# Scores of sliding-window attention: three one-bank PSUM tiles and a shared bank in place of two two-bank tiles

## The chip, the cores and the metric

One core of a Trainium2 chip runs the whole program. The metric is the device time of one execution in microseconds (us), lower is better. PE is TensorE (matmuls), DVE is VectorE, ACT is ScalarE, POOL is GpSimd, SP is SyncE, whose queue issues most of the DMAs. PSUM, into which PE writes, has eight banks of 512 fp32 columns for each partition, and this program uses all eight.

## The reference

Two independent layers whose outputs are put side by side: attention with a sliding window of 256 keys, and a Fourier mixing layer made of matrix products.

```python
q, k, v = (x @ wqkv)                      # 2048 tokens, 32 heads of 32
scores = q @ k.T * 32 ** -0.5
mask = (idx[:, None] - idx[None, :] >= 0) & (idx[:, None] - idx[None, :] < 256)
p = softmax(where(mask, scores, -1e9))
a = (p @ v) @ wo
b = dft_seq_re @ (xb @ dft_hid_re.T) - dft_seq_im @ (xb @ dft_hid_im.T)
out = concatenate([a, b], axis=-1)
```

## The kernel before

Every large product is made of fp16 matmuls on high and low halves of the fp32 operands, three passes each (`PASSES`). The first third of the program computes q, k and v; then come the products of the Fourier layer ("x" units, then "c" units by `seven`, four times over), and the output projection closes it.

Attention runs as a generator, `attention`, that is mixed into these products: each product calls `tick` after every 4 or 8 matmuls, and at a fixed rate the generator advances by one step. One block is a query block of 128 tokens and a pair of heads; there are 256 blocks, numbered b, ordered by head group, 512-token chunk, head pair and query block. `mm` chains all of these matmuls, so PE's order is the order in which the code is written, save for the small transposes (`pt_...`) behind the scale factors. DVE, ACT and SP order comes from the scheduler of the build, which simulates the program.

A block goes through these steps (lines of the profile):

- `s_step` (L205 to L249): PE writes the scores of two heads into a PSUM tile `s` (L222). A query block sees three key blocks: the two last ones, and the first one, of which the window cuts off one triangle, exactly the complement of the causal triangle of the diagonal block. So DVE copies the first key block's scores over the masked triangle of the diagonal block (L230, "the copy"); two key blocks' width is left. DVE takes the negative maximum (L232, `mx`), ACT makes the bias (L235), ACT writes the exponentials back into `s` (L242, one per head), ACT makes the high halves `hi` (L245), and DVE the low halves `lo` (L246), both into the tile `hl`. A transposing DMA (L248) turns `hl` into `t`.
- `z_step` (L260, L262), three blocks later, on POOL: the merged triangle is split again.
- `v_step`, `LAG` = 6 blocks later: PE multiplies by the values into `pv`; DVE normalises.

The tile `s` is 2 x 512 fp32, two banks, one per head, of which 3 x 128 columns each are used. The pool `ps_s` has two of them, so the matmuls of block b write where block b-2 stood, whose last reader is L246 on DVE. The first two query blocks of a sequence have one or two key blocks and no first key block to fold in; there the copy takes a constant (`never2`). Key blocks come from 512-token chunks (`k2s`, four key blocks each); a run of key blocks that crosses a chunk's edge needs two matmuls, one that does not needs one.

Around it, DVE also makes the low halves of the other operands (L115), the combinations of operands (L635) and of results (L683, L828).

## Time and profile before

| | |
|---|---|
| three runs | 1811.86, 1812.89, 1817.40 us; median 1812.89 |
| the profiled execution: its time | 1813.55 us |
| the profiled execution: its span, first to last instruction | 1811.5 us |
| mean granted TensorE clock | 0.989 |
| matmuls | 10876, of which 704 are scores (L222, recorded under the helper's line L108) |
| DMA | 297.95 MB, mean 164 GB/s |

The profile is one execution recorded by the hardware. A page sums each engine's busy time, groups instructions by line, operation and tile, and names what ended the idle time before them; other views list the waits, the chain of work that ended last, and the instructions in order of time. The helper `mm` stands at L108, so matmuls are told apart by tile names, with buffer numbers left out: `s` is the score tile, `p`, `p_a`, `p_b` and `p_c` are the Fourier products. In the timeline, rows read: start in us, duration in us, engine, line, operation, output<-input, shape, count of merged instructions, and in brackets the idle time before it and what ended it.

### The profile page before, as it was taken

What the parts mean: (1) busy time and instruction counts of PE and PEld (TensorE: products, weight loads), DVE (VectorE), ACT (ScalarE), POOL (GpSimd) and SP (SyncE); (2) the same over time, 40 slices, a digit from 0 to 9 for tenths busy, and PEclk for the clock granted to TensorE, in tenths of its full rate; (3) what the DMA queues carried; (4) which work ended last, traced back from release to release, by engine and by line L of the source; (5) the groups of instructions that cost most, each with busy time, mean ns of one, the idle gap of its engine ahead of it and who ended that gap; (6) DMA issues with size and microseconds to landing.
All of it is one profiled execution on the core that took longest, in us unless ns stands there. A gap on an engine that the chain in (4) does not pass through costs nothing.

```text
span 1811.5 us, 30024 instructions
## 1 busy us (share of the span) xinstructions
PE 1751.8 (97%) x10876; PEld 854.7 (47%) x10876; DVE 1327.5 (73%) x2362; ACT 1103.1 (61%) x1867; POOL 423.8 (23%) x666
## 2 busy tenths in 40 slices
PE   7999999999999999999989999999999989997999
PEld 3444445555555544554444444444444544443444
DVE  7666787777766788886788887779777778586542
ACT  3233555456555777876778876678776767563222
POOL 0000222122212232332244343324442234000000
PEclk9999999999999999999999999999999999998999
DMA  5357998978866666877657999847999747744431
GB/s 232 124 166 212 222 252 214 230 177 210 195 141 164 137 132 158 188 193 193 125 116 174 207 190 199 170 97 155 189 187 180 150 85 135 217 93 78 132 94 70
DMA packets 440596, 297.95 MB, mean 164 GB/s; under 512 B 339072, under 2 KB 396416, under 8 KB 440448
## 3 DMA queue, kind: packets, MB, share of 16 engines
q1 hardware_dynamic: 433536, 270.87, 63.8%
q0 software_dynamic: 6912, 25.17, 8.0%
q8 instruction: 85, 1.39, 0.3%
q14 instruction: 63, 0.52, 0.1%
HBM read 146.93 MB, written 75.63 MB: 123 GB/s over the span
## 4 chain that ended last, share of the span: by engine, by line
PE 75%; DVE 14%; ACT 5%; issue 3%; DMA 2%; POOL 0%; SPq 0%; ACTq 0%; DVEq 0%; POOLq 0%
PE p_a L108 12%; PE pv L108 12%; PE p L108 11%; PE pk L108 9%; PE pq L108 9%; PE p_b L108 6%; PE po_a L108 5%; PE s L108 4%; PE p_c L108 3%; PE po_b L108 2%; DVE reg L683 2%; DVE mx L232 1%; DVE raw_u L635 1%; PE po_c L108 1%; DVE reg L115 1%
## 5 line engine op out<-in xcount | busy, mean ns | idle before, releaser
L108 PE MATMUL p<-reg,un 128*128 128x512 f16 x1536 | 353.3, 382 | 2.5 <-ACT reg L826 2.5
L242 ACT ACTIVATE s<-s,bias,escs 128x256 f32<-128x256 f32 (+1 forms) x512 | 270.0, 527 | 12.2
L235 ACT ACTIVATE bias<-mx,pshift,escs 128x2 f32<-128x2 f32 x256 | 98.3, 384 | 258.4 <-DVE mx L232 257.6
L239 POOL TENSOR_SCALAR mark<-bias 128x1 f32<-128x1 f32 x128 | 46.5, 363 | 831.9 <-ACT bias L235 816.2
L108 PEld LDWEIGHTS <-un 128*128 128x128 f16 x1536 | 147.3, 98 | 167.2 <-issue 8.0
L246 DVE TENSOR_TENSOR hl<-s,hl 128x512 f16<-128x512 f32 (+1 forms) x256 | 170.1, 664 | 73.8 <-ACT hl L245 72.4
L262 POOL TENSOR_SCALAR_AFFINE_SELECT t<-t 128x512 f16<-128x512 f16 x224 | 184.9, 891 | 0.1
L108 PE MATMUL pq<-reg,wu_q 128*128 128x512 f16 x768 | 176.7, 385 | 7.5 <-ACT reg L121 4.3
L108 PE MATMUL p_a<-reg,un_c 128*128 128x512 f16 x768 | 182.8, 383 | 0.0
L108 PE MATMUL pk<-reg,wu_k 128*128 128x512 f16 x768 | 174.6, 379 | 0.0
L108 PE MATMUL pv<-reg,reg 128*128 128x512 f16 x768 | 174.0, 379 | 0.0
L260 POOL TENSOR_SCALAR_AFFINE_SELECT z<-t 128x512 f16<-128x512 f16 x224 | 164.2, 754 | 41.4 <-DMA t<-hl 37.7
L232 DVE TENSOR_REDUCE mx<-s 128x2 f32<-128x512 f32 (+1 forms) x256 | 170.8, 667 | 3.3
L108 PEld LDWEIGHTS <-reg 128*128 128x128 f16 x1152 | 110.1, 97 | 121.8
L245 ACT ACTIVATE hl<-s 128x512 f16<-128x512 f32 (+1 forms) x256 | 148.9, 582 | 9.8 <-DMA t<-hl 3.8
L230 DVE COPY_PREDICATED s<-upper,s 128x256 f32<-128x256 uint32 x224 | 94.5, 422 | 72.7 <-PE s L108 72.3
L108 PE MATMUL s<-qk,qk 96*128 96x128 f16 (+2 forms) x704 | 121.7, 276 | 15.4 <-DVE hl L246 14.7
L108 PEld LDWEIGHTS <-un_b 128*128 128x128 f16 x768 | 73.3, 98 | 101.4 <-issue 11.4
L108 PEld LDWEIGHTS <-wu_q 128*128 128x128 f16 x768 | 74.9, 99 | 95.6 <-issue 13.2
L108 PEld LDWEIGHTS <-un_c 128*128 128x128 f16 x768 | 74.4, 99 | 86.3 <-issue 4.4
L108 PEld LDWEIGHTS <-un_a 128*128 128x128 f16 x768 | 73.8, 97 | 84.7 <-issue 5.8
L108 PEld LDWEIGHTS <-wu_k 128*128 128x128 f16 x768 | 73.4, 97 | 81.1
(174 smaller groups left out, 2855.7 us busy)
## 6 DMA issues: line engine op xcount, KB each, us to landing
raw_u<-in_cs_dram SPq DMA_DIRECT2D x64, 512.0 KB, 4.4
qk<-qs SPq DMA_DIRECT2D x192, 128.0 KB, 3.2
out_dram<-y POOLq DMA_DIRECT2D x36, 512.0 KB, 7.8
raw_u<-in_xb_dram SPq DMA_DIRECT2D x32, 512.0 KB, 4.0
vs<-yv SPq DMA_DIRECT2D x32, 260.0 KB, 2.7
vt<-vs SPq DMA_DIRECT2D x32, 260.0 KB, 3.4
raw_x<-in_xa_dram SPq DMA_DIRECT2D x16, 512.0 KB, 10.2
qs<-yq SPq DMA_DIRECT2D x32, 256.0 KB, 2.4
```

The costliest lines, as they stand in the source:

```text
L108: fixed[:] = [nc.tensor.matmul(*args, **kwargs)]
L115: latest[:] = [f(*args, **kwargs)]
L230: nc.vector.copy_predicated(s[:, :, 2 * P:3 * P], upper2, s[:, :, :P] if nb == 3 else never2)
L232: nc.vector.tensor_reduce(mx, sv, axis=AX.X, op=ALU.max, negate=True)
L235: nc.scalar.activation(bias, mx, AF.Identity, bias=pshift, scale=es)
L239: marks[:] = [nc.gpsimd.tensor_scalar(mark, bias[:, 0:1], 1.0, None, op0=ALU.mult)]
L242: nc.scalar.activation(sv[:, h], sv[:, h], AF.Exp, bias=bias[:, h:h + 1], scale=es)
L245: nc.scalar.activation(hi, sv, AF.Copy)
L246: behind[:] = [nc.vector.tensor_tensor(lo, sv, hi, op=ALU.subtract)]
L260: nc.gpsimd.affine_select(out=z, in_=pk, compare_op=ALU.is_gt, fill=0.0, base=0, pattern=[[0, 4], [-1, P]], channel_multiplier=1)
L262: nc.gpsimd.affine_select(out=pk, in_=pk, compare_op=ALU.is_ge, fill=0.0, base=0, pattern=[[0, 4], [1, P]], channel_multiplier=-1)
L683: nc.vector.tensor_tensor(lo, src, hi, op=ALU.subtract)
```

## The change

The score tile becomes one bank: 2 heads x 256 columns, for the last two key blocks. There are three of them in place of two. The first key block gets a tile of its own, `far`, one bank for the whole program, 2 x 2 x 128 columns: one half for even blocks and one for odd ones, and in each half one part per head. The matmuls of a head are cut where the chunk ends, as before, and now also between the first key block and the two last ones. The copy reads from `far` and writes into `s`. The sum of banks stays at eight.

```diff
-    ps_s_cm = tc.tile_pool(name="ps_s", bufs=2, space=PSUM)
+    ps_s_cm = tc.tile_pool(name="ps_s", bufs=3, space=PSUM)
...
+        far = ps_s.tile([P, 2, 2, P], F32, tag="far", bufs=1, name="far")
...
-                st[b] = {"s": ps_s.tile([P, 2, 512], F32, tag="s", name=f"s_{b}")}
+                st[b] = {"s": ps_s.tile([P, 2, 2 * P], F32, tag="s", name=f"s_{b}")}
+                if nb == 3:
+                    st[b]["far"] = far[:, b % 2]
...
-            k0 = qb + 1 - nb
-            while k0 <= qb:
-                k1 = min(qb + 1, (k0 // QB + 1) * QB)
-                at = (k0 - (qb - 2)) * P
-                mm(s[:, j, at:at + (k1 - k0) * P], q2s[g, sc][:, h, i * P:i * P + P],
-                                 k2s[g, k0 // QB][:, h, k0 % QB * P:k0 % QB * P + (k1 - k0) * P],
-                                 start=True, stop=True, skip_group_check=True)
-                k0 = k1
+            edges = [k for k in range(qb + 1 - nb, qb + 2) if k in (qb + 1 - nb, qb - 1, qb + 1) or k % QB == 0]
+            for k0, k1 in zip(edges, edges[1:]):
+                at = (k0 - (qb - 1)) * P
+                mm(d["far"][:, j] if at < 0 else s[:, j, at:at + (k1 - k0) * P],
+                   q2s[g, sc][:, h, i * P:i * P + P],
+                   k2s[g, k0 // QB][:, h, k0 % QB * P:k0 % QB * P + (k1 - k0) * P],
+                   start=True, stop=True, skip_group_check=True)
...
-            sv = s[:, :, 3 * P - w:3 * P]
-            nc.vector.copy_predicated(s[:, :, 2 * P:3 * P], upper2, s[:, :, :P] if nb == 3 else never2)
+            sv = s[:, :, 2 * P - w:]
+            nc.vector.copy_predicated(s[:, :, P:], upper2, d["far"] if nb == 3 else never2)
```

The scheduler's order moves with it. The places below are those of which the prediction speaks. The first is PE at block 250, whose three key blocks lie in one chunk; `qk0` are the queries (the weights), `qk1` the keys, `p1_55` a product around it, and a bracket names the semaphores for which an instruction waits. Before:

```order
L108 LDWEIGHTS qk0_7_3_17080 [waits DVE_49]
L108 MATMUL s_250_17480<-qk1_7_3_17076,qk0_7_3_17080 128x384 [waits PE_49]
L108 LDWEIGHTS qk0_7_3_17080
L108 MATMUL s_250_17480<-qk1_7_3_17076,qk0_7_3_17080 128x384
L108 LDWEIGHTS un55_17210
```

and in the changed program:

```order
L108 LDWEIGHTS qk0_7_3_17416
L108 MATMUL far_379<-qk1_7_3_17412,qk0_7_3_17416 128x128 [waits DVE_49]
L108 LDWEIGHTS qk0_7_3_17416
L108 MATMUL s_250_17823<-qk1_7_3_17412,qk0_7_3_17416 128x256 [waits Activation_49]
L108 LDWEIGHTS qk0_7_3_17416
L108 MATMUL far_379<-qk1_7_3_17412,qk0_7_3_17416 128x128
L108 LDWEIGHTS qk0_7_3_17416
L108 MATMUL s_250_17823<-qk1_7_3_17412,qk0_7_3_17416 128x256
L108 LDWEIGHTS un55_17547
```

Two matmuls have become four of the same total width. The DVE value that the first one waits for was that of `lo` of block b-2; it is now that of the copy of block b-1 in nearly every block, also where b and b-1 use different halves of `far`. The `s` tile's own wait goes back to block b-3.

The second is DVE where it serves blocks 247 to 249 (`hl_248` is `lo` of block 248, `mx_249` the maximum of block 249, the rows on `reg1_81`, `raw_u56` and `pv_242` other work). Before:

```order
L246 TENSOR_TENSOR hl_247_17321<-s_247_17309,hl_247_17321 128x512
L635 TENSOR_TENSOR raw_u56_0_16814<-raw_u56_0_16814,raw_u56_1_16763 128x512
L635 TENSOR_TENSOR reg1_81<-reg1_81 128x512
L298 TENSOR_REDUCE pv_242_17387<-pv_242_17387 128x128
L246 TENSOR_TENSOR hl_248_17374<-s_248_17362,hl_248_17374 128x512
L230 COPY_PREDICATED s_249_17424<-upper_88,s_249_17424 128x2x128
L301 TENSOR_TENSOR o_7_2_17256<-pv_242_17387,rs_242_17412 128x2x64
```

and in the changed program:

```order
L248 TENSOR_TENSOR hl_247_17662<-s_247_17648,hl_247_17662 128x512
L637 TENSOR_TENSOR raw_u56_0_17143<-raw_u56_0_17143,raw_u56_1_17090 128x512
L232 COPY_PREDICATED s_249_17767<-upper_88,far_379 128x2x128
L637 TENSOR_TENSOR reg1_81<-reg1_81 128x512
L300 TENSOR_REDUCE pv_242_17730<-pv_242_17730 128x128
L248 TENSOR_TENSOR hl_248_17717<-s_248_17703,hl_248_17717 128x512
L234 TENSOR_REDUCE mx_249_17773<-s_249_17767 128x2
```

The copy of block 249 now stands three instructions earlier. At block 199, the same place of another Fourier stage, it moves ahead of one instruction, `lo` of block 198:

```order
L637 TENSOR_TENSOR reg1_81<-reg1_81 128x512
L300 TENSOR_REDUCE pv_192_14362<-pv_192_14362 128x128
L232 COPY_PREDICATED s_199_14403<-upper_88,far_379 128x2x128
L248 TENSOR_TENSOR hl_198_14349<-s_198_14337,hl_198_14349 128x512
L303 TENSOR_TENSOR o_6_0_14363<-pv_192_14362,rs_192_14376 128x2x64
```

where before it stood behind it:

```order
L635 TENSOR_TENSOR reg1_81<-reg1_81 128x512
L298 TENSOR_REDUCE pv_192_14091<-pv_192_14091 128x128
L246 TENSOR_TENSOR hl_198_14078<-s_198_14068,hl_198_14078 128x512
L230 COPY_PREDICATED s_199_14132<-upper_88,s_199_14132 128x2x128
L301 TENSOR_TENSOR o_6_0_14092<-pv_192_14091,rs_192_14105 128x2x64
```

Elsewhere DVE's order is the same but for some fourteen stretches of a few to a hundred instructions, and POOL's is unchanged.

## The prediction

> **What bounds the kernel now.** I read the page's busy shares first, then the list of PE's waits, then the timeline around the longest of them.

> ```profile
> PE 1751.8 (97%) x10876; PEld 854.7 (47%) x10876; DVE 1327.5 (73%) x2362; ACT 1103.1 (61%) x1867; POOL 423.8 (23%) x666
> PE s L108 <- DVE hl L246: 14.7, 13, 4.0
> PE s L108 <- DVE top_u L115: 0.6, 1, 0.6
> PE p_b L108 <- DVE reg L683: 6.6, 4, 2.4
> 108.74 20.72 PE pk L108 x96
> L108 PE MATMUL pk<-reg,wu_k 128*128 128x512 f16 x768 | 174.6, 379 | 0.0
> ```

> PE sets the end: it is busy for 97% of the span. It can only gain by losing waits, or lose by more work or new waits. The second and third rows are all its waits at the score matmuls: 13 for `lo`, and one credited to a small DVE reduction. Of these, `lo` of block b-2 is what the change takes off the score tile's path. They understate the loss: a 512-column matmul shows 379 ns, but 96 of them in a row pass in 20.72 us, 216 ns each, so a row's end is drawn 0.163 us after the next could have begun. The stream therefore loses 15.3 + 14 x 0.163 = 17.6 us at the 14 waits. The two longest stand here, each as PE's rows with a copy (L230) or a `lo` (L246) next to them; rows of other work between them are left out.

> ```profile
> 1204.92 3.61 PE L108 MATMUL p<-reg,un 128*128 128x512 f16 x16
> 1205.32 0.42 DVE L230 COPY_PREDICATED s<-upper,s 128x256 f32<-128x256 uint32 x1
> 1211.42 0.49 PE L108 MATMUL s<-qk,qk 96*128 96x384 f16 x2 [2.88 <-DVE hl L246]
> 1211.74 5.30 PE L108 MATMUL p<-reg,un 128*128 128x512 f16 x16
> 1212.22 0.67 DVE L246 TENSOR_TENSOR hl<-s,hl 128x512 f16<-128x512 f32 x1
> 1212.82 0.41 DVE L230 COPY_PREDICATED s<-upper,s 128x256 f32<-128x256 uint32 x1
> 1216.88 0.49 PE L108 MATMUL s<-qk,qk 96*128 96x256 f16 x4
> ...
> 1474.65 0.41 DVE L230 COPY_PREDICATED s<-upper,s 128x256 f32<-128x256 uint32 x1
> 1480.26 0.67 DVE L635 TENSOR_TENSOR raw_u<-raw_u,raw_u 128x512 f32<-128x512 f32 x1
> 1480.39 0.82 PE L108 MATMUL s<-qk,qk 96*128 96x128 f16 x4 [3.99 <-DVE hl L246]
> 1482.39 0.41 DVE L230 COPY_PREDICATED s<-upper,s 128x256 f32<-128x256 uint32 x1
> 1488.53 0.49 PE L108 MATMUL s<-qk,qk 96*128 96x384 f16 x2
> ```

> They are blocks 199 and 249. PE had nothing to do for 2.88 and 3.99 us because DVE, with a queue of other work, reached `lo` of block b-2 late. Afterwards PE runs slowly: 16 matmuls take 5.30 us where 16 took 3.61 just before. The windows name the cause in the column behind POOL's, the granted clock:

> ```profile
> 1212.70:1216.10 3.40, 3.40 (x10) 1.22 (x9) 1.92 (x5) 0.93 (x2) 0.21 (x1) 0.50 0.97 197
> 1478.90:1485.70 6.80, 5.31 (x15) 2.17 (x16) 5.30 (x10) 3.70 (x8) 0.94 (x3) 0.50 0.40 77
> ```

> Half the clock for 3.40 us costs 1.70; for the 5.31 us in which PE worked in the second, 2.65. So the two longest waits cost 4.35 us more than the wait rows say.

> **The change, part by part.**

> *The wait for `lo` of b-2 goes.* A score tile now waits for block b-3, a whole block, about 5.3 us, further back (256 blocks start between 151.8 and 1517.1 us, the x704 row below); the longest wait was 4.0. Gain: 17.6 + 4.35 = 21.9 us, if nothing else holds PE.

> *A new wait, for the copy of b-1.* [...] Queued behind it are all later matmuls. At block 249 that copy had ended at 1474.65 + 0.41 = 1475.06; PE came there at 1480.39 - 4.15 = 1476.24, 1.2 us later. At block 199 it had ended at 1205.74, PE came at 1208.4. So at neither would this wait have replaced the old one. An ordinary block shows the usual room:

> ```profile
> 800.06 0.49 PE L108 MATMUL s<-qk,qk 96*128 96x256 f16 x4
> 800.39 1.03 PE L108 MATMUL p_b<-reg 128*128 128x512 f16 x4
> 801.35 0.42 DVE L230 COPY_PREDICATED s<-upper,s 128x256 f32<-128x256 uint32 x1
> 806.25 0.49 PE L108 MATMUL s<-qk,qk 96*128 96x128 f16 x4
> 811.00 0.49 PE L108 MATMUL s<-qk,qk 96*128 96x384 f16 x2
> 811.33 1.89 PE L108 MATMUL p_a<-reg,un_c 128*128 128x512 f16 x8
> ```

> and two rows on all score matmuls:

> ```profile
> L108 PE MATMUL s<-qk,qk x704: 217/272/528, 151.8 to 1517.1; 96*128 96x128 f16 x64, 96*128 96x384 f16 x64, 96*128 96x256 f16 x48
> L108 PE MATMUL s<-qk,qk 96*128 96x128 f16 x224 | 41.6, 220 | 5.8 <-DVE hl L246 5.8
> ```

> The copy ends at 801.77, the next scores start at 806.25: 4.5 us. The block after a removed wait is the dangerous one, because PE then arrives earlier while DVE is still behind. Block 200 would come 1211.42 - 3.04 + (5.46 - 1.70) = 1212.14 us, and the copy of 199 ended at 1213.23. The new order puts that copy ahead of one `lo` (0.60 us to the next start), so 1212.63: a wait of 0.5. Block 250 would come at 1476.24 + (8.14 - 2.65) = 1481.73; the copy of 249, now right behind the 1480.26 row, ends about 1481.3: none. I take 0.5 us; the bounds are 0 and, with the copies where they stand now, 1.1 + 1.1 = 2.2.

> *More matmuls.* A head's three key blocks took one matmul, or two at a chunk's edge, and now take two or three: 33 instead of 22 for the 16 query blocks of a head, 1056 instead of 704 in all, with as many more weight loads, and the same columns. The rows price the piece: the four-piece block runs from 800.06 to 800.39, the two-piece one from 811.00 to 811.33, 0.33 us both. To 0.01 us for two pieces it is at most 5 ns each, so 352 pieces cost 0 to 1.8 us; I take 0.9. The weight loads lie beside PE's stream, as in the four-piece block.

> [...]

> *The copy itself* reads another bank than it writes, which no row shows. The nearest rows are 422 ns for the copy now and 480 for its form with a constant:

> ```profile
> L230 DVE COPY_PREDICATED s<-upper,s 128x256 f32<-128x256 uint32 x224 | 94.5, 422 | 72.7 <-PE s L108 72.3
> L230 DVE COPY_PREDICATED_SCALAR s<-upper,never x32: 475/480/489, 152.9 to 1372.7; 128x256 f32 x32
> ```

> I take no difference, since the bytes and the engine are the same. At 60 ns more, 224 copies are 13 us of an engine that is idle for a quarter of the span; a tenth of that, 1.3 us, would reach PE in the stretches where DVE is full. If it were as much faster, the gain is as small. The maximum, the exponentials and `hi`/`lo` keep their shapes, and PE still writes a bank that no one reads.

> *What is late next.* PE will arrive earlier at other things that DVE makes. The p_b row above (6.6 us in 4 waits, for L683) has one of its waits at 1230.3 and one at 1501.7, each some 20 us behind a long wait that goes. Between them DVE can catch up only by its own idle time.

> ```profile
> 1230.30 0.59 PE L108 MATMUL p_b<-reg,un_b 128*128 128x512 f16 x2 [1.04 <-DVE reg L683]
> 1501.68 0.59 PE L108 MATMUL p_b<-reg,un_b 128*128 128x512 f16 x2 [1.28 <-DVE reg L683]
> ```

> The windows give DVE's busy time in between (third busy column), and the rows under them its longest waits there:

> ```profile
> 1211.40:1228.90 17.50, 17.14 (x99) 8.22 (x99) 13.38 (x25) 13.25 (x25) 1.69 (x3) 0.90 0.56 129
> DVE s L230 <- PE s L108: 2.8, 1, 2.8
> 1480.40:1500.00 19.60, 19.60 (x106) 9.33 (x107) 13.67 (x26) 13.33 (x25) 3.48 (x7) 0.86 0.38 82
> DVE hl L246 <- ACT hl L245: 3.2, 2, 2.3
> DVE s L230 <- PE s L108: 2.3, 2, 1.9
> 932.70:948.50 15.80, 15.27 (x94) 7.37 (x95) 14.97 (x28) 14.60 (x28) 5.27 (x8) 1.00 0.82 166
> ```

> In the first window PE gets 3.04 + 1.70 - 0.5 = 4.2 us earlier, DVE is idle for 17.50 - 13.38 = 4.1, of which 2.8 are spent waiting for PE's scores and so can go: 1.4 us come back as a wait there. In the second PE gets 6.8 earlier; DVE's idle time is 5.9, of which 2.3 wait for scores and 3.2 for ACT's `hi`, which partly follows the scores; I let 4.1 go, halfway between 2.3 and 5.9: 2.7 come back. After the wait at 932 DVE is idle for 0.8 of 15.8 us while PE gets 1.2 earlier; 0.4 come back at least, and I take 0.8 for this and the smaller ones. Together 4.9; the bounds are 0 and the whole gain.

> *Sum* against the profiled execution's own 1813.55 us, 0.7 above the median of the runs, 1812.89: -21.9 + 0.5 + 0.9 + 4.9 = -15.6, so 1798.0. The 2 us between span and time stay.

> **The rivals.**

> *The waits only move.* DVE is the one that is late; if its lateness goes on to the next operand, the gain shrinks to the clock and the few waits at which DVE has slack. For it: the full DVE of the third window. Against it: DVE's own idle time is mostly a wait for PE, `72.3` of `72.7` us before the copies in their row above. With four fifths of 21.9 coming back: about 1810.

> *The copy becomes the gate (slower).* One buffer for the first key block ties block b to the copy of b-1, where two tiles gave two blocks' time. The place is 920 to 1240 us, the dense Fourier stages, 320 / 5.3 = 60 blocks. It decides once the copies there run some 4.5 us later than the one at 801, six DVE instructions of 0.7 us. If each of the 60 blocks then waits 0.5 us, that is 30 us against 21.9 gained: 1822. Against it: the copy's room, 1.2 us at the worst of the places above, while PE was late by a lot more.

> *Short matmuls cost a weight load.* A weight load takes 98 ns, a 128-column matmul a quarter of 216, 54:

> ```profile
> L108 PEld LDWEIGHTS <-un 128*128 128x128 f16 x1536 | 147.3, 98 | 167.2 <-issue 8.0
> ```

> If the load set the pace of a short piece, each extra one would cost the other 44 ns, 352 x 44 = 15.5 us in place of 0.9, and the time would be 1812.6. The equal 0.33 us of two and four pieces speak against it; only that the pieces of `far` alternate with those of `s` is new. [...]

> **How the numbers follow.** Forecast 0.74, waits only move 0.12, copy as gate 0.11, short matmuls 0.03. The forecast's own range is 1791 (all 21.9 kept, 1813.55 - 21.9) to 1807. The range for 8 in 10 reaches up to the second case, 1790 to 1812. A difference of 0.3%, 5.4 us, is what a measurement of this kernel can tell from no change: faster is below 1807.5, slower above 1818.3. The forecast and a part of the short-matmul and moved-wait cases lie below, the rest of these within, the gate above but for a tail: 0.77 faster, 0.14 the same, 0.09 slower.

> **What would show it.** In the profile after, PE's waits at scores for `lo` should be gone, and any wait of PE at `far` should be for a copy, under 2 us in all. Half-clock windows near 1212 and 1479 should vanish. PE's waits for L683 and L115 operands should grow by about 5 us. The score blocks should still take 0.33 us in full width. I am wrong if the waits for copies sum to more than 5 us, if a piece costs over 10 ns, or if the waits for DVE's other products grow by as much as the scores' waits shrink.

## The result, and the profile after

| | before | changed |
|---|---|---|
| median of four runs each, us | 1814.32 (1811.86 to 1817.40) | 1796.13 (1795.28 to 1797.33) |
| ratio of times, with its 95% interval | | 0.9899 [0.9881, 0.9917] |
| profiled execution: time, span, us | 1813.55, 1811.5 | 1796.02, 1794.3 |

The changed kernel is faster by 18.2 us, 1.0%; 1798.0 was predicted. The code lines behind the edit now have numbers two higher (L230 is L232, L246 is L248, L683 is L685, L828 is L830). First, from the page of the changed kernel, the engines' busy time:

```profile
PE 1748.1 (97%) x11228; PEld 871.9 (49%) x11228; DVE 1327.8 (74%) x2362; ACT 1101.1 (61%) x1867; POOL 423.6 (24%) x666
```

PE has 352 matmuls more than before and yet 3.7 us less busy time, DVE the same work to 0.3 us. So what went is not work. The list of PE's waits in the changed kernel (total us, times, longest) shows what it is; rows that differ from before's by 0.7 us or less, and that the argument does not need, are left out:

```profile
PE p_b L108 <- DVE reg L685: 8.6, 4, 2.6
...
PE p_a L108 <- DVE y L830: 3.8, 3, 1.9
PE pt_u L156 <- DVE top_u L115: 3.3, 5, 1.1
...
PE p L108 <- ACT reg L828: 0.8, 1, 0.8
...
PE far L108 <- DVE s L232: 0.4, 1, 0.4
```

The rows that answer to these in the list of before, where that of L683 was 6.6 in 4:

```profile
PE p_a L108 <- DVE y L828: 3.9, 4, 1.9
...
PE pt_u L156 <- DVE top_u L115: 2.6, 4, 1.1
PE p L108 <- ACT reg L826: 2.5, 1, 2.5
```

No wait for `lo` is left: 14.7 us in 13 waits are gone, and with them the 0.6 us that had been put down to `top_u` at the scores. One wait for a copy has come, 0.4 us. Of the rows shown two have grown, L685 by 2.0 and `top_u` by 0.7, and one has shrunk by 1.7, an ACT product that the edit does not touch. Over all rows PE's waits went from 55.3 us in 49 to 41.9 us in 37.

Whose time that was is read from the waits of DVE, with before's two rows first and the changed kernel's two behind them:

```profile
DVE s L230 <- PE s L108: 80.7, 79, 2.8
DVE hl L246 <- ACT hl L245: 72.4, 57, 3.3
```

```profile
DVE s L232 <- PE s L108: 73.4, 73, 2.6
DVE hl L248 <- ACT hl L247: 63.6, 52, 2.7
```

DVE does the same work in 17.2 us less span. The two waits that hang on PE's scores, its own for the scores and the one for ACT's product of them, gave up 7.3 + 8.8 = 16.1 us. DVE's queue was late at `lo` and then had to wait for the scores that its lateness had held back; the third score tile broke that circle.

The single copy wait, in the timeline of the changed kernel, is at the matmuls of block 200 (rows of other work left out):

```profile
1203.58 0.41 DVE L232 COPY_PREDICATED s<-upper,far 128x256 f32<-128x256 uint32 x1
...
1204.05 0.22 PE L108 MATMUL far<-qk,qk 96*128 96x128 f16 x1 [0.35 <-DVE s L232]
```

The copy of block 199 ends at 1203.99 and PE starts right behind it. The pieces can be read at an ordinary block of the changed kernel:

```profile
809.12 0.22 PE L108 MATMUL far<-qk,qk 96*128 96x128 f16 x1
...
809.46 1.89 PE L108 MATMUL p_a<-reg,un_c 128*128 128x512 f16 x8
```

Four matmuls alternate between `far` and `s` and the next product starts 0.34 us after the first of them; before, that was 0.33 for two. The two half-clock windows at 1212.7 and 1478.9 have gone, but there are three others. In the windows of the changed kernel the granted clock is the column behind POOL's:

```profile
945.40:948.80 3.40, 1.03 (x6) 0.50 (x5) 3.40 (x6) 2.87 (x6) 3.40 (x5) 1.00 0.81 216
948.80:952.20 3.40, 3.40 (x13) 1.57 (x13) 2.77 (x9) 2.48 (x4) 0.37 (x1) 0.50 0.95 125
...
1218.50:1221.90 3.40, 3.37 (x19) 1.51 (x19) 2.44 (x8) 2.00 (x4) 0.47 (x1) 0.50 0.23 46
1484.70:1488.10 3.40, 3.40 (x31) 1.86 (x30) 2.42 (x8) 3.05 (x6) 0.80 (x2) 0.50 0.03 6
```

Each comes behind one of the waits for L685, which stand in the timeline of the changed kernel as

```profile
948.73 0.96 PE L108 MATMUL p_b<-reg,un_b 128*128 128x512 f16 x2 [2.37 <-DVE reg L685]
...
1218.53 1.01 PE L108 MATMUL p_b<-reg,un_b 128*128 128x512 f16 x2 [2.60 <-DVE reg L685]
...
1484.47 0.81 PE L108 MATMUL p_b<-reg,un_b 128*128 128x512 f16 x2 [1.68 <-DVE reg L685]
```

The first of these waits stood in the profile of before too, 2.35 us for L683 up to 951.23, and there the clock stayed whole. What differs is where the wait fell. In the record of the granted clock, the half-clock windows of one profile start at whole multiples of 3.413 us from each other: at 948.82, 1218.47 and 1484.71 in the changed kernel, which is 79 and 78 such steps, and at 14.60, 1212.68 and 1478.92 before, 351 and 78 steps. So each execution has its own grid of steps. In the changed kernel the wait, from 946.4 to 948.7, lies inside one step, the one from 945.4, in which PE worked for 1.03 us. On the grid of before it lies across an edge, at 949.85, and neither step is as empty:

```profile
946.44:949.85 3.41, 2.44 (x12) 1.11 (x11) 3.41 (x5) 3.38 (x8) 2.08 (x4) 1.00 0.78 200
949.85:953.26 3.41, 2.03 (x12) 1.08 (x12) 3.41 (x9) 2.37 (x4) 1.82 (x2) 1.00 0.94 174
```

The clock also differs at the start of the program, where the edit does nothing. Before, then changed:

```profile
14.60:18.00 3.40, 2.77 (x7) 0.98 (x7) 3.40 (x4) 2.38 (x3) 0.00 (x0) 0.50 1.03 411
41.90:48.70 6.80, 5.54 (x13) 1.82 (x13) 6.29 (x6) 3.60 (x4) 0.00 (x0) 0.50 0.17 54
```

```profile
14.60:18.00 3.40, 2.52 (x13) 1.16 (x13) 3.40 (x4) 2.62 (x3) 0.00 (x0) 1.00 1.03 412
44.30:47.70 3.40, 3.40 (x10) 1.21 (x8) 3.40 (x4) 0.79 (x1) 0.00 (x0) 0.50 0.01 2
```

Half of 2.77 + 5.54 against half of 3.40: 2.5 us of the two profiles' difference lie there. A stretch of 10.24 us at half clock near the end holds less of PE's work than before, then changed:

```profile
1639.34:1649.58 10.24, 6.30 (x15) 2.02 (x16) 7.43 (x9) 2.99 (x4) 0.00 (x0) 0.50 0.47 106
```

```profile
1621.25:1631.49 10.24, 4.60 (x11) 1.44 (x12) 9.14 (x11) 2.66 (x3) 0.00 (x0) 0.50 0.58 128
```

Half of 6.30 against half of 4.60 is 0.9 us. The account of the 17.2 us of span is then: waits 55.3 - 41.9 = 13.4, with 12 x 0.163 = 2.0 for the ends that are drawn too late; start of the program 2.5; half clock in the middle 5.1 (half of 3.40 + 3.37 + 3.40) against 4.35 before, so -0.75; half clock near the end 0.9; pieces -0.9, as the prediction took them. The sum is 17.1.

### The profile page after: what moved, and what is told of

Same layout as the page of the kernel before. It is cut to its first block, busy times and chain, and to the rows that moved or that the text cites. A ratio compares the mean times of both kernels' runs of the same rounds, so it can differ in the third digit from the quotient of the medians.

```text
span 1794.3 us, 30681 instructions
## 1 busy us (share of the span) xinstructions
PE 1748.1 (97%) x11228; PEld 871.9 (49%) x11228; DVE 1327.8 (74%) x2362; ACT 1101.1 (61%) x1867; POOL 423.6 (24%) x666
## 4 chain that ended last, share of the span: by engine, by line
PE 81%; DVE 11%; ACT 4%; issue 2%; DMA 1%; SPq 0%; ACTq 0%; DVEq 0%
PE p_a L108 17%; PE pv L108 13%; PE p L108 9%; PE pk L108 9%; PE pq L108 9%; PE p_b L108 8%; PE po_a L108 5%; PE p_c L108 4%; PE s L108 3%; PE po_b L108 2%; DVE reg L685 2%; PE far L108 1%; PE po_c L108 1%; DVE mx L234 1%; DVE y L637 1%
## 5 line engine op out<-in xcount | busy, mean ns | idle before, releaser
L108 PE MATMUL p<-reg,un 128*128 128x512 f16 x1536 | 349.3, 379 | 0.8 <-ACT reg L828 0.8
L241 POOL TENSOR_SCALAR mark<-bias 128x1 f32<-128x1 f32 x128 | 51.3, 401 | 821.0 <-ACT bias L237 804.6
L108 PEld LDWEIGHTS <-un 128*128 128x128 f16 x1536 | 146.3, 97 | 157.9 <-issue 1.1
L248 DVE TENSOR_TENSOR hl<-s,hl 128x512 f16<-128x512 f32 (+1 forms) x256 | 170.4, 666 | 66.8 <-ACT hl L247 63.6
L108 PE MATMUL p_a<-reg,un_c 128*128 128x512 f16 x768 | 185.3, 387 | 0.0
L108 PE MATMUL pq<-reg,wu_q 128*128 128x512 f16 x768 | 174.4, 381 | 8.2 <-ACT reg L121 4.3
L108 PE MATMUL pk<-reg,wu_k 128*128 128x512 f16 x768 | 174.4, 379 | 0.0
L108 PE MATMUL pv<-reg,reg 128*128 128x512 f16 x768 | 174.0, 379 | 0.0
L108 PEld LDWEIGHTS <-reg 128*128 128x128 f16 x1152 | 110.3, 98 | 118.9
L232 DVE COPY_PREDICATED s<-upper,far 128x256 f32<-128x256 uint32 x224 | 94.7, 423 | 66.6 <-PE s L108 66.2
L108 PEld LDWEIGHTS <-un_b 128*128 128x128 f16 x768 | 73.4, 98 | 102.5 <-issue 12.8
L108 PEld LDWEIGHTS <-wu_q 128*128 128x128 f16 x768 | 74.4, 98 | 93.5 <-issue 11.1
L108 PEld LDWEIGHTS <-qk 96*128 96x128 f16 x1056 | 88.6, 98 | 63.1 <-issue 1.7
L108 PEld LDWEIGHTS <-un_c 128*128 128x128 f16 x768 | 75.2, 99 | 85.7 <-issue 6.7
L108 PEld LDWEIGHTS <-un_a 128*128 128x128 f16 x768 | 73.8, 97 | 83.1 <-issue 6.1
L108 PE MATMUL p_b<-reg,un_b 128*128 128x512 f16 x384 | 95.0, 390 | 17.9 <-DVE reg L685 8.6
```

The lines of the kernel that those rows point to most:

```text
L108: fixed[:] = [nc.tensor.matmul(*args, **kwargs)]
L232: nc.vector.copy_predicated(s[:, :, P:], upper2, d["far"] if nb == 3 else never2)
L241: marks[:] = [nc.gpsimd.tensor_scalar(mark, bias[:, 0:1], 1.0, None, op0=ALU.mult)]
L248: behind[:] = [nc.vector.tensor_tensor(lo, sv, hi, op=ALU.subtract)]
```

## The experiments

They ran on three chips, each with the kernel before beside them: e1 to e5 (before 1816.66 us, 27 runs), e6 to e9 (1814.40, 17 runs), e10 and e11 (1815.38, 17 runs). Ratios are to before on the same chip.

### Only the new bank, with two score tiles

```diff
-    ps_s_cm = tc.tile_pool(name="ps_s", bufs=3, space=PSUM)
+    ps_s_cm = tc.tile_pool(name="ps_s", bufs=2, space=PSUM)
```

> The change with two score tiles in place of three; far stays, one bank. Theory (the gain is the third tile, which moves the wait for lo back by a block): PE waits for lo of b-2 again, 13 to 18 waits at score matmuls with 14 to 18 us in all, and the time is that of before plus the pieces and the copy wait, 1812 to 1818 us. Rival (the gain comes from the new order of DVE and ACT, or from the shorter tile): near 1796 us, with few waits at scores.

Measured (e1): 1814.29 us, ratio 0.9986 [0.9972, 1.0001]. From the list of PE's waits of this kernel:

```profile
PE s L108 <- DVE hl L248: 13.1, 12, 3.6
```

With `far`, the pieces and the new copy, but two tiles, the waits for `lo` are back and the gain is gone. The gain is the third tile.

### Only the pieces, in the kernel before

The tile of two banks and the copy stay; a head's matmuls are cut between the first key block and the two last.

```diff
-            k0 = qb + 1 - nb
-            while k0 <= qb:
-                k1 = min(qb + 1, (k0 // QB + 1) * QB)
+            edges = [k for k in range(qb + 1 - nb, qb + 2) if k in (qb + 1 - nb, qb - 1, qb + 1) or k % QB == 0]
+            for k0, k1 in zip(edges, edges[1:]):
...
-                k0 = k1
```

> Before, with the score matmuls cut between the first key block and the two last ones, and nothing else: 1056 score matmuls in place of 704. Theory: 0 to 1.8 us more than before, score blocks still 0.33 us, waits for lo unchanged. Rival (a short piece costs its weight load): 10 to 16 us more.

Measured (e2): 1812.71 us, ratio 0.9982 [0.9967, 0.9997]; its waits for `lo` come to before's sum, 14.7 us, in 11 waits in place of 13; the second row is spoken of below:

```profile
PE s L108 <- DVE hl L244: 14.7, 11, 3.6
...
PE p L108 <- ACT reg L824: 0.8, 1, 0.8
```

The 352 matmuls cost nothing that can be seen; the time even came out 0.5 to 6 us lower. Part of that may be the second row, the ACT product for which PE had waited 2.5 us: it fell to 0.8 here too, though the edit has nothing to do with it. The cause of that row was not traced. A weight load that sets the pace (10 to 16 us more) is ruled out: the interval of the ratio ends at 0.9997.

### Four score tiles and no wait for the copy, two ways

`far` is dropped, and its bank becomes a fourth score tile. The first key block's matmuls write into the diagonal block's columns and are overwritten there, so they cost PE the same (a matmul of 128 columns at the score tile takes 219 ns in the first of the two kernels, one at `far` 220 in the changed kernel); the copy takes other data, the first time from SBUF, the second time from the score tile itself. In both kernels the first key block's scores are left out of the result.

```diff
-    ps_s_cm = tc.tile_pool(name="ps_s", bufs=3, space=PSUM)
+    ps_s_cm = tc.tile_pool(name="ps_s", bufs=4, space=PSUM)
...
-                mm(d["far"][:, j] if at < 0 else s[:, j, at:at + (k1 - k0) * P],
+                mm(s[:, j, P:] if at < 0 else s[:, j, at:at + (k1 - k0) * P],
...
-            nc.vector.copy_predicated(s[:, :, P:], upper2, d["far"] if nb == 3 else never2)
+            nc.vector.copy_predicated(s[:, :, P:], upper2, ident.unsqueeze(1).to_broadcast([P, 2, P]) if nb == 3 else never2)
```

> Four one-bank score tiles and no far: the first key block's matmul writes into the diagonal block's columns and is overwritten, and the copy takes a constant matrix, so the first key block's scores are left out of the result; every instruction keeps its count and shape. There is no wait for the copy of b-1 and the tile's own wait goes back to b-4. Theory: the copy wait cost 0.5 us, so 1795 to 1797 us, within 1.5 us of the change. Rival (the shared far bank gives back a good part of the gain): 5 us or more below the change.

Measured (e3): 1805.94 us, ratio 0.9945 [0.9927, 0.9963], by the ratios some 8 us slower than the changed kernel. Neither theory had that. The group of copies in this kernel (busy us, mean ns) and the wait that grew most:

```profile
L229 DVE COPY_PREDICATED s<-upper,ident 128x256 f32<-128x256 uint32 x224 | 114.0, 509 | 67.7 <-PE s L108 67.3
```

```profile
PE p_a L108 <- DVE y L827: 7.6, 8, 1.9
```

The copy from SBUF took 509 ns where the one from `far` takes 423, 86 x 224 = 19.3 us more of DVE. Whether it was that or the four tiles, the second kernel tells, whose copy reads PSUM (its edit against the first):

```diff
-            nc.vector.copy_predicated(s[:, :, P:], upper2, ident.unsqueeze(1).to_broadcast([P, 2, P]) if nb == 3 else never2)
+            nc.vector.copy_predicated(s[:, :, P:], upper2, s[:, :, :P] if nb == 3 else never2)
```

> Four score tiles and no far, as in the earlier run with four tiles, but the copy takes its data from the score tile itself in PSUM and not from a constant in SBUF, where it took 509 ns in place of 423; the first key block's scores are left out of the result. Theory (the 19 us of DVE work that the slower copies added made that run slow, not the tiles): copies at 423 ns, within 2 us of the change. Rival (a fourth tile lets the score work crowd DVE's other work): again 7 to 11 us above the change.

Measured (e7): 1796.60 us, ratio 0.9907 [0.9883, 0.993]; copies of this kernel:

```profile
L229 DVE COPY_PREDICATED s<-upper,s 128x256 f32<-128x256 uint32 x224 | 94.5, 422 | 68.9 <-PE s L108 68.8
```

That is the time of the changed kernel, 1797.71 us on the same chip (e6, below). A fourth tile and the freedom from the wait for the copy are worth nothing that these runs show, and the loss of the first version came with its copies from SBUF. Most likely it is their 19.3 us of DVE; but POOL was busy for 436.5 us there and for 422.8 in the second version, with the same instructions, and no run parts the two.

### Holding attention back where DVE is late

The four waits for L685 stand where an x stage passes into a c stage. This kernel takes no attention steps during the last x unit and the first two positions of the first c unit, and makes them up afterwards at half as much again as the usual rate.

```diff
+    hold, debt = [False], [0.0]
...
-        acc[0] += n * rate
+        inc = n * rate
+        if hold[0]:
+            debt[0] += inc
+            return
+        more = min(debt[0], inc * 0.5)
+        debt[0] -= more
+        acc[0] += inc + more
...
+                hold[0] = k == 3 and bool(pair)
...
+            hold[0] = i == 0
...
-                  lambda turn: hook(n, turn))
+                  lambda turn: (hook(n, turn), hold.__setitem__(0, i == 0 and turn < 1)))
```

> The change, with the attention steps held back while PE runs the last x unit of a Fourier stage and the first two positions of the first c unit, and made up at half again the rate afterwards. Theory (what PE waits for now is DVE's L685 rows, late because the score work of attention stands among them): the L685 waits, 8.6 us in 4, fall under 3 us, a half-clock window or two goes with them, 1786 to 1793 us. Rival (DVE is full over the whole stage, so waits only move): the same waits turn up at scores, pv or other operands after the hold, 1796 us or more.

Measured (e5): 1801.15 us, ratio 0.9916 [0.989, 0.9941]. PE's waits in this kernel:

```profile
PE p_a L108 <- DVE y L837: 8.1, 5, 5.7
...
PE s L108 <- DVE hl L248: 3.6, 3, 1.9
PE p_b L108 <- DVE reg L692: 3.3, 3, 1.2
```

The waits aimed at fell from 8.6 to 3.3; 4.3 came up at `p_a`, 3.6 at the scores and 5.1 in waits for POOL's rows and for a copy at `far`. Nothing is gained; here waits do move.

### The change again, and one half of `far` for all blocks

The first kernel (e6) is the changed one, unaltered; the second (e8) differs in one place:

```diff
-                    st[b]["far"] = far[:, b % 2]
+                    st[b]["far"] = far[:, 0]
```

> The change itself, with before beside it on the chip of the other runs of this set. Theory: the ratio of its first result, 0.988 to 0.992. Rival (part of that ratio was one chip's chance): 0.994 or more.

> The change with one half of far for all blocks. Theory (the two halves are one bank and one wait, so they buy nothing): the same instruction order, within 1 us of the change. Rival (the alternate half lets PE run ahead of the copy of b-1): 3 us or more above, with waits for copies at far.

Measured: 1797.71 us, ratio 0.9911 [0.9888, 0.9935], and 1795.92 us, ratio 0.9912 [0.9885, 0.9939]. The result repeats in this second set of runs, and the two halves buy nothing: block b waits for the copy of block b-1 whether it uses the same half or the other, and in both profiles PE waits at `far` once, for 0.4 us. The prediction took this wait from the order of the changed program, and the times agree; no run tells whether it comes from the two halves lying in one bank or from `far` being one tile.

### The copy made twice

```diff
             nc.vector.copy_predicated(s[:, :, P:], upper2, d["far"] if nb == 3 else never2)
+            nc.vector.copy_predicated(s[:, :, P:], upper2, d["far"] if nb == 3 else never2)
```

> The change with the copy made twice in each block: 256 more instructions of DVE, 224 x 0.42 + 32 x 0.48 = 110 us, and the result unchanged. Theory (DVE decides what is late next, but only in its dense stretches, about a tenth of its work): 8 to 20 us more, as longer waits of PE for DVE's rows at L685, L830 and for copies. Rival (DVE's idle quarter hides it): less than 4 us more. Rival (DVE sets the pace after the change): 50 us or more.

Measured (e9): 1817.65 us, ratio 1.0015 [0.9997, 1.0034], 19.9 us over the changed kernel on the same chip. Its waits:

```profile
PE far L108 <- DVE s L233: 8.1, 7, 2.8
PE p_b L108 <- DVE reg L686: 7.6, 4, 2.2
PE p_a L108 <- DVE y L831: 6.2, 6, 1.9
...
PE pt_u L156 <- DVE top_u L115: 5.7, 7, 1.7
```

The rows of the second copies sum to 94.4 us (224 at 421 ns) and 15.4 us (32 constant ones). Rows of DVE that stand close are drawn overlapping, so its busy time rose by less, from 1328.1 us in e6 to 1420.7, 92.6 us, and of these 0.21 us per us came through to the end. PE's waits at `far` rose from 0.4 to 8.1 us: the rival in which the copy is the gate exists. But this kernel also holds `far` longer, because the second copy stands behind other rows, 0.9 us after the first in the median and up to 4.0; how much of the 8.1 us comes from that and how much from the fuller DVE no run tells.

### Work taken from DVE

One (e10), then two (e11) of the combinations of operands at L637 go to POOL in each c unit:

```diff
-            sub(r2[:, :4], r2[:, :4], r2[:, 4:], ALU.add)
+            nc.gpsimd.tensor_tensor(r2[:, :4], r2[:, :4], r2[:, 4:], op=ALU.add)
```

```diff
-            sub(r1[:, :4], r1[:, :4], r2[:, :4])
-            sub(r2[:, :4], r2[:, :4], r2[:, 4:], ALU.add)
+            nc.gpsimd.tensor_tensor(r1[:, :4], r1[:, :4], r2[:, :4], op=ALU.subtract)
+            nc.gpsimd.tensor_tensor(r2[:, :4], r2[:, :4], r2[:, 4:], op=ALU.add)
```

> The change with one of the four L637 operand combinations of each c unit (128 x 512 fp32, 0.68 us, 32 units, 22 us of DVE) moved from DVE to POOL, which is busy for 24% of the span; the result is the same. Theory (DVE work is worth about 0.2 us of time per us after the change, as the double copy showed): 2 to 6 us below the change, 1790 to 1795 us. Rival (POOL is slower, its steps for attention come later, or the operand itself is late): the same or more, 1797 us and up, with new waits of PE for POOL's rows or for the operands behind them.

> The same with two of the four combinations on POOL, 44 us of DVE. Theory: 5 to 10 us below the change. Rival: POOL's chain sets the end of the operands, more than the one-combination kernel and more than the change.

Measured: 1798.41 us, ratio 0.9906 [0.9879, 0.9932], and 1813.40 us, ratio 0.9982 [0.9964, 0.9999]. In the first of the two kernels, the moved group on POOL and its remaining partner on DVE:

```profile
L668 POOL TENSOR_TENSOR raw_u<-raw_u 128x512 f32<-128x512 f32 x32 | 47.0, 1469 | 115.1 <-DVE raw_u L637 97.5 <-issue 17.7
...
L637 DVE TENSOR_TENSOR raw_u<-raw_u,raw_u 128x512 f32<-128x512 f32 x96 | 70.0, 729 | 9.2 <-POOL raw_u L668 8.3
```

The same groups in the second kernel, and its longest wait of PE:

```profile
L667 POOL TENSOR_TENSOR raw_u<-raw_u,raw_u 128x512 f32<-128x512 f32 x32 | 49.4, 1543 | 76.0 <-DVE un_a L115 67.6 <-DVE rs L298 8.5
...
L637 DVE TENSOR_TENSOR raw_u<-raw_u,raw_u 128x512 f32<-128x512 f32 x64 | 47.7, 746 | 15.9 <-POOL raw_u L668 15.1
```

```profile
PE p_a L108 <- DVE y L830: 11.6, 9, 3.3
```

An addition of 729 ns on DVE takes 1469 on POOL, and DVE stands 8.3 us waiting for it; with two of them moved it stands 15.1 us, and PE's wait for `y` at `p_a`, 3.8 us in the changed kernel, is 11.6. DVE also became lighter by much less than the 22 and 44 us that were moved: its busy time is 1319.1 and 1318.6 us against 1327.8. In the second kernel the 32 rows that make `reg` from `raw_u` (L115) took 1248 ns each where the changed kernel takes 754; why was not traced. So these runs do not show what a DVE lighter by 22 us would give; they show that moving the additions to POOL does not give it. No version beat the changed kernel.

## Why the prediction was right, point by point

*The waits for `lo`* (-17.6): right. They are gone, and with two tiles (e1) they return together with the time.

*The new wait, for the copy* (+0.5): right in size and place. It was predicted at block 200 and only there, 0.5 us; it stands there, 0.35 drawn and 0.16 for the drawn end, and is the only one. That block 250 would not wait held too. In e7 no block waits for a copy, and the time is the same within what can be told.

*The pieces* (+0.9): right within what can be told. The block's start to the next product's start went from 0.33 to 0.34 us, and e2 shows no cost.

*The clock* (-4.35): this term was mis-sized. The prediction said that the half-clock windows "near 1212 and 1479 should vanish", and they did, but it took them as gone for good. Three windows of 3.4 us came up behind the waits for L685 and cost 5.1, so the term was +0.75 in this execution. The step that failed is the one that put down the half clock behind the two longest waits as a gain, and none behind the waits that it expected to grow. Two executions with the same wait, the first of the changed kernel run again (e6), the second of the kernel with one half of `far` (e8), show that the length of a wait does not settle it:

```profile
950.36 0.95 PE L108 MATMUL p_b<-reg,un_b 128*128 128x512 f16 x2 [2.36 <-DVE reg L685]
...
951.74 2.95 PE L108 MATMUL p_a<-reg,un_c 128*128 128x512 f16 x8
```

```profile
950.55 0.59 PE L108 MATMUL p_b<-reg,un_b 128*128 128x512 f16 x2 [2.37 <-DVE reg L685]
...
951.31 1.89 PE L108 MATMUL p_a<-reg,un_c 128*128 128x512 f16 x8
```

Behind 2.36 us the eight matmuls took 2.95 us, behind 2.37 us they took 1.89. Again the grids differ. In e6 a half-clock window starts at 950.47, and the wait lies inside the step before it; in e8 one starts at 1218.88, and 79 steps of 3.413 us back from there an edge, at 949.23, cuts the wait in two:

```profile
947.05:950.46 3.41, 1.05 (x6) 0.53 (x5) 3.41 (x6) 2.86 (x6) 3.41 (x5) 1.00 0.85 222
```

```profile
945.82:949.23 3.41, 2.36 (x12) 1.04 (x11) 3.41 (x6) 3.38 (x8) 2.17 (x4) 1.00 0.98 238
949.23:952.65 3.42, 2.10 (x15) 1.15 (x15) 3.42 (x10) 2.36 (x4) 1.76 (x2) 1.00 0.93 180
```

Where the grid lies against the wait is chance: behind a wait of 2.35 to 2.37 us at this place, half clock came in three of five profiles (changed, e6 and e7; not in before and e8). The term should have been an average over that chance for every wait of this size, before and after. An estimate from the limit read in the last section, between 1.95 and 2.15 us of a step without PE: with 2.0 for it, a wait of 2.36 us draws half clock at (2.36 + 3.41 - 2 x 2.0) / 3.41 = 0.5 of the positions, before's 2.88 at 0.7 and its 3.99 at all of them.

*What is late next* (+4.9): mis-sized too, the other way. L685 gained 2.0 and `top_u` 0.7, together 2.7 where 4.9 were taken. By place, the wait at 1230.30 before, 1.04 us, is 2.60 in the changed kernel, 1.6 more where 1.4 were worked out. The wait at 1501.68, 1.28 us, is 1.68, and 0.6 more came up just before it, 1.0 where 2.7 were worked out. That second place is the size that failed, the "I let 4.1 go" of DVE's idle time. In the changed kernel's stretch that answers to it, DVE is idle for 0.8 us where it was 5.9, and its wait for ACT's `hi`, 3.2 us before, which the prediction let go only in part, is 0.7:

```profile
1464.50:1482.40 17.90, 17.35 (x113) 8.72 (x112) 17.10 (x32) 15.36 (x30) 7.01 (x9) 1.00 0.44 97
DVE hl L248 <- ACT hl L247: 0.7, 1, 0.7
```

In PE's list the ACT product lost 1.7 and smaller rows gained 0.5, so that all of the list but the waits at `s` and at `far` stands at +1.5. It is luck that the two errors, 5.1 one way and 3.4 the other, in part cancel. Whoever counts the half-clock windows with the waits behind which they stand gets 1.5 + 5.1 = 6.6 for this term and -4.35 for the clock, and both terms are then right to 1.7 us. The whole sum, -15.6, stands against -17.2 of span, of which 2.5 are the clock's chance at the start and 0.9 the half clock near the end, which no term foresaw.

*The copy itself* (0): right, 423 ns from the other bank against 422. The price put on a slower one, "a tenth of that", was too low: in e9 0.21 of the added DVE time came through, some of it perhaps by the longer hold on `far`, and in e3, against e7 by their ratios, (0.9945 - 0.9907) x 1815 = 7 of 19.3 us, about a third, though the two intervals touch. At a third the upper bound of this term would have been 4 to 5 us instead of 1.3.

*The rivals.* "The waits only move" did not hold for this change, since DVE's idle time, from which it caught up, had been waits for PE's scores and for ACT's product of them; it did for e5, where a stall was pushed about without any slack being won. "The copy becomes the gate" is a real mechanism by e9, but cost 0.4 us in the change itself. "Short matmuls cost a weight load" is refuted by e2.

## What to carry to other kernels

Where an engine with a quarter of its time idle makes the bound engine wait, look at what that idle time waits for: if it is the bound engine's own product, one more buffer between the two can take out the whole stall, and here one buffer was enough (a fourth tile gave nothing). Bytes of a buffer may be had by splitting off a part that lives shorter: the first key block's scores are dead after one copy, and a single bank for them sufficed although all blocks share it. Before moving work off a late engine, ask whether that engine will then stand waiting for the result. And price a stall with the half clock that it can draw, as a chance and not as a certainty.

## What the runs showed of the hardware

```profile
1209.27:1212.68 3.41, 1.26 (x7) 0.66 (x7) 3.41 (x6) 2.16 (x4) 0.00 (x0) 1.00 0.02 4
1120.52:1123.93 3.41, 1.46 (x7) 0.68 (x7) 1.33 (x3) 1.83 (x4) 0.12 (x1) 1.00 1.16 265
```

They leave PE 3.41 - 1.26 = 2.15 and 3.41 - 1.46 = 1.95 us without work.

A predicated copy of 128 x 256 fp32 into PSUM took 422 ns with its data in PSUM in the tile that it writes (before and e7), 423 from another bank (the changed kernel), and 509 ns with its data in SBUF (e3, a 128 x 128 tile read twice). No run tells the place from the repeated reading.

An fp32 `TENSOR_TENSOR` of 128 x 512 took 1469 to 1543 ns on POOL and 729 to 746 on DVE in the same kernels (e10 and e11).
